# Six query chunks in place of five, a last head set in two halves, and a PSUM bank for P·V taken at its first product, in a fused attention and MLP block

## The chip, the cores and the metric

The kernel runs on one core of one Trainium2 chip. A core has five engines that run side by side, each in the order of its own program: TensorE (PE; its weight loads, PEld, overlap its products), VectorE (DVE), ScalarE (ACT), GpSimd (POOL) and SyncE (SP, which here only issues DMAs). They meet through semaphores. PE writes into PSUM, here eight banks of 128 partitions x 512 fp32; the other data lies in SBUF. The metric is the device time of one execution in microseconds, median of several runs.

## The reference

A transformer block with adaptive layernorm: 2048 tokens, width 640, 32 heads of 20, an MLP of width 1536 with a bilinear gate.

```python
mod = (silu(c) @ w_mod).reshape(c.shape[0], 6, 1, -1)
sa, ca, ga, sb, cb, gb = (mod[:, 0], mod[:, 1], mod[:, 2], mod[:, 3], mod[:, 4], mod[:, 5])
h = layernorm(x) * (1 + ca) + sa
q, k, v = split_heads(h @ wqkv)                 # 32 heads of 20
p = softmax(einsum('bhqd,bhkd->bhqk', q, k) * 20 ** -0.5)
x = x + ga * (merge_heads(einsum('bhqk,bhkd->bhqd', p, v)) @ wo)
h = layernorm(x) * (1 + cb) + sb
x = x + gb * (((h @ w_gate) * (h @ w_up)) @ w_down)
```

## The kernel before

The program is not written out by hand. `build_kernel` makes tasks (engine, estimated duration, dependencies, priority, and at times a gate), and `Sched` plays them through in a list simulation on the host; the order in which it starts them on each engine becomes that engine's instruction stream (`emit_program`), with semaphore waits where a task depends on another engine. So every number of the planner sets an order, and a task that comes late on the chip delays all that stands behind it on its engine.

*Queries* are worked in chunks (`CHUNKS`: 512, 512, 512, 256, 256). Heads go in sets of four, so there are 5 x 8 = 40 items (chunk, head set), in that order. For an item the scores of all 2048 keys are needed. The work is cut into units of 128 keys x 512 queries, or 256 keys x 256 queries (two products side by side, L1480): 64 units for an item of a 512-query chunk and 32 for one of 256. Four heads sit in four 32-row groups of PE's array.

*Exponentials* are made in two ways. Most units go in pairs through ScalarE: one call reads two banks of scores (sets A and B, banks 0 and 1, 3 and 4) and writes bf16 probabilities into a ring `PP` (L1517; `score_q`, one group for each call, NG groups). The others, in quads of four units whose number for each item is in `QUADS` (108 in all), are made by VectorE from the bits of a scaled score: L1541 reads one score bank into `DB`, L1573 and L1581 cut out mantissa and exponent, and L1578 (VectorE) or four pieces of L1593 (GpSimd) multiply; this gives two terms, so P·V runs twice for such a unit. Their scores ride along with a score group (`d_attach`) when their due time (`D_LEAD`, `DL`) has come.

*P·V* (L2038, `pv_issue`) sums over all keys of an item into one PSUM bank, fixed: `BPV` = 7. V carries a column of ones, so the softmax sum comes along. When the last product of an item is done, VectorE transposes the bank into `OT` (L1665, T1), takes reciprocals (L1669), GpSimd normalises (L1671, VectorE for the last item), VectorE transposes back into `OcT` (L1679), and SP copies the heads' rows into `Ocp` (L1692). Only then may the next item's first P·V product start: `st_pv["free"]`.

*After an item row* (all eight sets of a chunk) `suffix` makes the chunk's MLP part: output projection with `wo` (for the last chunk the last head set's part comes straight from `OcT` with `wo7`), residual add into `xck` (L1763), statistics and layernorm (L1777 to L1784; the power -0.5 on GpSimd, L1782), transposes (L1796) with scale and shift into `h2T` (L1801 or L1803), twelve rounds of gate and up with weights that stream through three buffers `stg` (L1836), or that lie ready in `stx` for the last chunk, gate copied to `gsb` and multiplied into `hprod` (L1858 to L1896), and the down products (wd) with a final add (L1919) and the store (L1928). On PE this is all filler ("X" rounds) between score groups: `pick_pe` takes a score group when its banks are free, else P·V candidates, else X rounds by priority, where gates (`GATE_F`) keep a round back until so many exponential groups are out. X rounds and VectorE's score units share the PSUM banks `G` = 5, 6, 2. Dummy products (`do_fill`, L2405; `zero_fill`, L2377) are put in where the recent PE activity falls under `FILL_MIN` or `FILL_Z`. The last chunk's gate and up and down products use the whole array (L935); all others are split in four column groups (L939).

*At the start* x is loaded, normalised, transposed, and projected: K, Q directly or as packed rows that go through DRAM (`kq_round`, `packed_round`; `K_ALL`, `Q_DIRECT`, `LATEQ`), V in two parts of 320 columns (`V_PARTS`, `v_round`, L1288 casts).

`STAGE` overrides planner constants for one item after the other, by item number.

Of the kernel before, what the change touches and what calls it, by code (L numbers as in the profile page):

```python
# [12 lines left out]
SEM = 60.0  # L13
# [21 lines left out]
class Task:  # L35
    __slots__ = ("head", "hval", "hknow", "eng", "dur", "lat", "deps", "emits", "ctr", "prio", "gate", "acq", "on_start", "slots",
                 "start", "done", "needed", "val", "know", "nleft", "ready", "users", "name", "mode", "seq", "rt", "sem",
                 "nbytes", "cond", "alt", "land", "lk")

    def __init__(self, eng, dur, emits, deps=(), ctr=None, prio=0.0, lat=None, gate=0, acq=(), on_start=None,  # L40
# [26 lines left out]
        self.lk = 0  # L67
        if lat is None:
            lat = {"pe": PE_DRAIN, "act": ACT_LAT, "dve": DVE_LAT, "pool": 60.0}.get(eng, 0.0)
        self.lat = lat  # L70

# [49 lines left out]
class Sched:  # L121
# [32 lines left out]
    def locked(self, eng, task):  # L154
# [4 lines left out]
        if task.lk == 2:  # L159
            tt = max(self.t, self.free_at["dve"])  # L160
            for d in sorted(self.readyl["dve"], key=lambda x: (x.prio, x.seq)):
# [89 lines left out]
    def pull(self, eng):  # L251
        p = self.pend[eng]
        while p and p[0][0] <= self.t:
            _, _, task = heapq.heappop(p)
            self.readyl[eng].append(task)

    def step_engine(self, eng):
# [4 lines left out]
        rl.sort(key=lambda x: (x.prio, x.seq))  # L262
        for k, task in enumerate(rl):
            if task.gate > self.progress or (task.cond is not None and not task.cond()):
                continue
# [12 lines left out]
    def steal(self):  # L278
# [4 lines left out]
        for task in self.readyl["dve"]:  # L283
            if task.alt is not None and (best is None or (task.prio, task.seq) < (best.prio, best.seq)):
                best = task
        if best is None or self.free_at["dve"] <= self.t and best is min(self.readyl["dve"], key=lambda x: (x.prio, x.seq)):
# [41 lines left out]
def emit_program(nc, sched, nsem_dma=56):  # L328
# [97 lines left out]
    with nc.Block() as block:  # L426
# [20 lines left out]
        def _(e):  # L447
# [4 lines left out]
CHUNKS = ((0, 512), (512, 512), (1024, 512), (1536, 256), (1792, 256))  # L452
QUADS = ((0, 4, 3, 3, 3, 4, 4, 4),
# [35 lines left out]
K_ALL = (0,)  # L489
# [6 lines left out]
V_PARTS = [[0, 4], [4, 8]]  # L496
# [24 lines left out]
OPFIRST = 0  # L521
# [4 lines left out]
LATEQ = (3,)  # L526
LATEQ_A = 2
LATEQ_F = 0.534
# [4 lines left out]
    0: {"X_LATE": -179.96, "D_RES": 74, "EAGER": 9, "PVMAX": 14, "HOLD": 95, "PVTOL": 249, "D_LATE": 16, "PVMIN": 2, "PVCAP": 12, "FILL_MIN": 4190.746, "TPRIO": 0.75, "XDPRIO": 1.343, "XBACK": 0, "STEAL_GAP": 200, "FILL_Z": 3300.0, "Z_LATE": 0.0},  # L533
    1: {"HOLD": 91, "D_LATE": 10, "PVMAX": 7, "Z_LATE": 89.79, "FILL_MIN": 4705.4},
    2: {"DL": 0.376, "D_LATE": 17, "D_RES": 29, "FILL_Z": 3209.68, "EAGER": 9, "FILL_MIN": 4297.75},
# [1945 lines left out]
```

## Time and profile before

| | us |
|---|---|
| median of 3 runs | 811.79 |
| runs | 810.24 to 813.02 |
| profiled execution: span | 809.0 |
| first exponential (L1517) starts | 16.13 |
| last exponential ends | 770.19 |
| PE busy from 16.1 to 770.2 in dummy products L2405 | 27.5 |
| longest idle of ScalarE before 770 (35.80, after a score) | 1.29 |

The profiled execution is one execution with the profiler on; its span runs from the first to the last instruction. In the stretches shown below each engine's busy time stands with its number of instructions in brackets, then the granted TensorE clock as a share of full speed, the busy share of the DMA engines and GB/s. In a timeline a row has start, duration, engine, line, operation, what it writes and reads, its count, and in square brackets how long the engine had been idle and what ended that. Two successive instructions of one engine overlap, so a mean duration is longer than the step from one to the next.

### The profile page before, as it was taken

The numbers are of one execution on the slowest core, as the hardware profiler recorded it, in microseconds if no ns is written. First come the engines' busy times: TensorE is split into PE (matmuls) and PEld (weight loads), VectorE is DVE, ScalarE is ACT, GpSimd is POOL, SyncE is SP. The second block draws the span as 40 slices with busy tenths as digits, with TensorE's granted clock in tenths as the row PEclk, the third lists the DMA queues.
The fourth block names the chain that finished last, engine by engine and source line by source line (L and its number), as shares of the span: only waits on it lengthen the run. The fifth ranks groups of instructions, "written<-read, shape, count | busy, mean of one in ns | idle before, by whom it ended". The sixth has DMA issues, their size and how long they took to land.

```text
span 809.0 us, 29314 instructions
## 1 busy us (share of the span) xinstructions
PE 792.6 (98%) x12585; PEld 303.1 (37%) x12585; DVE 703.1 (87%) x1273; ACT 763.8 (94%) x853; POOL 321.2 (40%) x330
## 2 busy tenths in 40 slices
PE   9999999999999999999999999999999999999998
PEld 4433333222232333233233232343244433444567
DVE  7979987999999999999998999999699875778973
ACT  7899999999999999999999999999999999999912
POOL 3304244565524442164335334444265340443520
PEclk9999999999999999999999999999999999999999
DMA  9633211113330144100301221001201236005520
GB/s 306 210 87 105 71 46 42 47 36 123 91 67 25 40 112 132 26 9 20 85 25 31 48 57 30 11 22 53 56 6 31 55 78 144 23 30 125 115 70 17
DMA packets 116447, 54.74 MB, mean 68 GB/s; under 512 B 83915, under 2 KB 116319, under 8 KB 116319
## 3 DMA queue, kind: packets, MB, share of 16 engines
q1 hardware_dynamic: 115391, 51.72, 24.3%
q8 instruction: 100, 1.64, 0.8%
q10 hardware_dynamic: 928, 1.15, 0.4%
q14 instruction: 28, 0.23, 0.1%
HBM read 41.85 MB, written 8.41 MB: 62 GB/s over the span
## 4 chain that ended last, share of the span: by engine, by line
PE 52%; ACT 34%; DVE 8%; issue 4%; SPq 1%; DMA 0%; POOL 0%; ACTq 0%; POOLq 0%
ACT PP L1517 34%; PE ps_all L1480 17%; PE ps_all L939 15%; PE ps_all L2038 11%; DVE DB L1541 3%; PE ps_all L935 3%; PE ps_all L1199 3%; PE ps_all L1135 1%; PE ps_all L2403 1%; DVE DSS L1581 1%; DVE DSS L1578 1%; PE ps_all L2405 1%; DVE DSS L1573 1%; PE ps_all L1096 1%; DVE wd L1463 0%
## 5 line engine op out<-in xcount | busy, mean ns | idle before, releaser
L1517 ACT ACTIVATE PP<-ps_all 128x1024 bf16<-128x1024 f32 x808 | 743.9, 1144 | 5.2 <-PE ps_all L1480 4.4
L1593 POOL TENSOR_TENSOR DSS<-DB,DSS 128x512 bf16<-128x512 bf16 x224 | 254.9, 1156 | 324.6 <-DVE DSS L1581 236.0
L1541 DVE TENSOR_SCALAR DB<-ps_all 128x512 int16<-128x512 f32 x432 | 288.5, 684 | 45.0 <-PE ps_all L1480 42.2
L1480 PE MATMUL ps_all<-QT,KT 32*128 32x512 bf16 (+1 forms) x2560 | 315.7, 340 | 8.3 <-ACT PP L1517 5.9
L1480 PEld LDWEIGHTS ps_all<-QT,KT 32*128 32x128 bf16 x2560 | 82.4, 91 | 266.3 <-ACT PP L1517 230.0
L2038 PE MATMUL ps_all<-PP,Vf 128*32 128x512 bf16 (+1 forms) x2032 | 158.8, 343 | 0.3 <-DVE OT L1665 0.3
L939 PE MATMUL ps_all<-h2T,stg 128*32 128x512 bf16 (+1 forms) x1744 | 118.1, 345 | 1.2 <-DVE DB L1541 0.9
L2038 PE MATMUL ps_all<-DSS,Vf 128*32 128x512 bf16 (+2 forms) x1056 | 84.4, 343 | 0.4 <-POOL DSS L1593 0.2
L1573 DVE TENSOR_SCALAR DSS<-DB 128x2048 int16<-128x2048 int16 x108 | 75.5, 699 | 0.5
L1581 DVE TENSOR_SCALAR DSS<-DB 128x2048 int16<-128x2048 int16 x108 | 75.8, 702 | 0.0
L2038 PEld LDWEIGHTS ps_all<-PP,Vf 128*32 128x32 bf16 x2032 | 44.6, 94 | 78.4 <-issue 72.1
L1671 POOL TENSOR_TENSOR OTn<-OT,invT 128x512 bf16<-128x512 f32 (+1 forms) x39 | 37.8, 970 | 89.4 <-DVE invT L1669 89.3
L1578 DVE TENSOR_TENSOR DSS<-DB,DSS 128x2048 bf16<-128x2048 bf16 x52 | 67.1, 1290 | 0.2
L939 PE MATMUL ps_all<-wd,hprod 128*32 128x320 bf16 (+1 forms) x1348 | 60.1, 282 | 0.0
L939 PEld LDWEIGHTS ps_all<-h2T,stg 128*32 128x32 bf16 x1744 | 37.2, 95 | 35.7 <-issue 23.6
L939 PEld LDWEIGHTS ps_all<-wd,hprod 128*32 128x32 bf16 x1348 | 29.7, 96 | 19.7 <-issue 11.3
L2038 PEld LDWEIGHTS ps_all<-DSS,Vf 128*32 128x32 bf16 (+1 forms) x1056 | 26.4, 95 | 19.7 <-issue 8.2
L939 PE MATMUL ps_all<-wV,hT 128*32 128x320 bf16 (+1 forms) x692 | 31.7, 291 | 0.0
L1885 DVE CAST gsb<-ps_all 128x512 bf16<-128x512 f32 x36 | 24.5, 680 | 8.1 <-PE ps_all L939 8.0
L1199 PE MATMUL ps_all<-hT,wq 128*32 128x512 bf16 x375 | 31.5, 382 | 0.0
L1665 DVE STREAM_TRANSPOSE OT<-ps_all 128x512 f32<-128x512 f32 (+1 forms) x40 | 24.1, 603 | 7.3 <-PE ps_all L2038 7.3
L939 PE MATMUL ps_all<-wo,Ocp 128*32 128x320 bf16 (+1 forms) x648 | 29.8, 283 | 0.6 <-DVE DB L1541 0.2
(124 smaller groups left out, 531.6 us busy)
## 6 DMA issues: line engine op xcount, KB each, us to landing
stg<-in_B_w_gate_dram SPq DMA_DIRECT2D x50, 160.0 KB
stg<-in_B_w_up_dram SPq DMA_DIRECT2D x50, 160.0 KB
QT<-q_rows SPq DMA_DIRECT2D x22, 128.0 KB
KT<-k_rows SPq DMA_DIRECT2D x84, 32.0 KB
wm<-in_w_mod_dram SPq DMA_DIRECT2D x3, 800.0 KB
x<-in_A_x_dram SPq DMA_DIRECT2D x7, 320.0 KB
xck<-in_A_x_dram SPq DMA_DIRECT2D x3, 640.0 KB
wd<-in_B_w_down_dram SPq DMA_DIRECT2D x1, 1920.0 KB
```

Of the source, the lines that this page charges most:

```text
L939: return lambda e, b: e.matmul(ps[32 * x:32 * x + 32, b, c0 + o:c0 + o + w], lhs()[:, 32 * x:32 * x + 32], rhs() if w == n else rhs()[:, o ...
L1199: f = [lambda e, b_, k=k, x=x: e.matmul(ps[x:x + min(32, w - x), b_, :], wx[:, k, r0 + x:r0 + min(x + 32, w)], hT[tc][:, k, :], tile_posit ...
L1480: ems.append(lambda e, i=i, kt=kt: e.matmul(dstf()[:, i * u.n:(i + 1) * u.n], KT[32 * u.s:32 * u.s + 32, u.j, kt * 128:(kt + 1) * 128], QT ...
L1517: return e.activation(PPs[g % 2][:, cellp["p"], 0:nu * 512], ps[:, b0:b0 + nu, :].rearrange("p b c -> p (b c)"), AFT.Exp, scale=ESCALE)
L1541: return e.tensor_scalar(DBl[st_["slot"]][:, x * 512:(x + 1) * 512], bank(cell["b"]), EBIAS, 0.0, op0=ALU.add, op1=ALU.max)
L1573: return e.tensor_scalar(DSl[st_["ss"][0]][:, :], DBl[st_["slot"]][:, :], 0x7F, 0x3F00, op0=ALU.bitwise_and, op1=ALU.bitwise_or)
L1578: return e.tensor_tensor(d, DBl[st_["slot"]][:, :].bitcast(BF16), d, ALU.mult)
L1581: return e.tensor_scalar(DSl[st_["ss"][1]][:, :], DBl[st_["slot"]][:, :], 0x7F80, 2, op0=ALU.bitwise_and, op1=ALU.bitwise_or)
L1593: return e.tensor_tensor(d, DBl[st_["slot"]][:, x * w:x * w + w].bitcast(BF16), d, ALU.mult)
L1671: f3 = lambda e: e.tensor_tensor(OTn[:, 0:n].rearrange("p (b c r) -> p b r c", c=32, r=2), OT[:, 0:n].rearrange("p (b r c) -> p b r c", c= ...
L1885: f = lambda e: e.tensor_copy(gsb[:, gs, 0:n], ps[:, r.b["b"], 0:n])
L2038: ems.append(lambda e, i=i, kt=kt, stt=stt, stp=stp: e.matmul(ps[32 * s:32 * s + mc, BPV, 0:u.n], Vf[:, (kt * H + 4 * u.j + s) * VW:(kt * ...
```

## The change

The chunks become 512, 512, 256, 256, 256, 256 with a new `QUADS` (104 quads in all). The last chunk's last head set is made as two items of 128 queries (units of four products of 128 keys x 128 queries), without quads; the output projection, layernorm, transposes, gate/up and down of the last chunk are made for each 128-query tile by itself. The bank for P·V is no longer fixed: bank 7 joins the pool `G`, an item takes a bank when its first P·V product is issued, and the next item may start while the one before is still open (`PV_OPEN`), if `PV_KEEP` banks are free. V is made in four parts of 160 columns. Odd chunks get a second residual buffer `xckb`. The output projection comes earlier in priority (`OPFIRST`), the rows of K for the first 512 tokens are no longer made directly (`K_ALL`), two query blocks come late (`LATEQ`), zero fills are gone, `GATE_F` and `STAGE` are rewritten (the latter from 40 rows of many overrides to some 30 rows of few). The scheduler's own lists are kept sorted, and abandoned alternatives are marked dead; this is host work.

```diff
-CHUNKS = ((0, 512), (512, 512), (1024, 512), (1536, 256), (1792, 256))
-QUADS = ((0, 4, 3, 3, 3, 4, 4, 4),
-         (3, 5, 2, 4, 3, 4, 4, 4),
-         (4, 2, 4, 4, 4, 4, 4, 4),
-         (1, 2, 1, 2, 2, 1, 1, 2),
-         (0, 2, 1, 1, 3, 0, 3, 2))
+CHUNKS = ((0, 512), (512, 512), (1024, 256), (1280, 256), (1536, 256), (1792, 256))
+QUADS = ((0, 4, 3, 3, 3, 4, 4, 4), (3, 5, 2, 4, 3, 4, 4, 4), (2, 1, 2, 1, 2, 1, 2, 1), (2, 1, 2, 1, 2, 1, 2, 1), (2, 2, 1, 2, 2, 2, 1, 2), (2, 1, 2, 2, 2, 1, 2, 0))
+SPLITJ = 1
+QHALF = ((0, 0), (0, 0))
+TB_GATE = 2
+PV_W4 = 430.0
+PV_OPEN = 2
+PV_KEEP = 2
...
-K_ALL = (0,)
+K_ALL = ()
...
-V_PARTS = [[0, 4], [4, 8]]
+V_PARTS = [[0, 2], [2, 4], [4, 6], [6, 8]]
...
-GATE_F = (0.446, 0.693, 0.969, 0.658, 1.0)
+GATE_F = (0.446, 0.6, 0.5, 0.5, 0.5, 1.0)
...
-FILL_Z, Z_LATE = 3300.0, 0.0
...
-OPFIRST = 0
+OPFIRST = 1500
...
-LATEQ = (3,)
-LATEQ_A = 2
-LATEQ_F = 0.534
+LATEQ = (2, 3)
+LATEQ_A = -20
+LATEQ_F = 0.35
...
+    xckb = at("xckb", [128, 4, D], BF16, qt_off)
...
-    G = Slots([5, 6, 2] if HEADG else [5, 6], "G")
+    G = Slots([5, 6, 2, 7], "G")
...
-    BPV = 7
...
+    if SPLITJ:
+        del items[-SPLITJ:], spans[-SPLITJ:], nqs[-SPLITJ:]
+        for hf in range(2):
+            for x in range(SPLITJ):
+                items.append((NC - 1, NSET - SPLITJ + x))
+                spans.append((128 * hf, 128))
+                nqs.append(QHALF[hf][x])
...
+        xfree = outs_r[ci % 2] + v_last
+        if ci % 2 and not alt:
+            xck = xckb
+            xfree = outs_r[1] + sfx_done["qd0"] + x0_done
...
+                gt = gate(KD * 320)
+                if early and SPLITJ:
+                    gt = NG - TB_GATE
...
+            for tl in range(ntl):
+                for f2 in range(0, FT, 2):
+                    mms = []
+                    for w_ in range(2):
+                        for x in range(2):
+                            cell = gu_w[f2 + x][0][w_]
+                            for k in range(KD):
+                                f = full(128, lambda k=k, cell=cell: cell["t"][:, k, :],
+                                         lambda k=k, tl=tl: h2T[:, k, tl * 128:(tl + 1) * 128], k == 0, k == KD - 1,
+                                         256 * w_ + 128 * x)
+                                mms.append((C128, f))
...
     def pv_candidates(t, maxn):
-        it = st_pv["item"]
-        if it >= len(items):
-            return []
-        for d in st_pv["free"]:
-            if d.done is None or d.done + SEM > t:
-                return []
...
+        for it in range(st_pv["item"], min(len(items), st_pv["item"] + PV_OPEN)):
+            info = item_info[it]
+            if info["bank"] is None:
+                ga = G.avail()
+                if ga is None or ga[0] > t or it > st_pv["item"] and len(G.free) < PV_KEEP:
+                    break
...
+            if info["bank"] is None:
+                info["bank"], rel = G.take(G.avail()[1], 1)
+                deps = deps + rel
```

More of the change, by code (lines that the diff above doesn't have):

```diff
@@ L70, in __init__, with KEY @@
         self.lat = lat
+def KEY(x):
+    return (x.prio, x.seq)
 class Slots:
@@ L1933, in suffix @@
         bd["tr"] = tr_l[-1:]
-        bd["out"] = outs
+        if not alt:
+            outs_r[ci % 2] = outs
     t1s = {}
@@ L2031, in pv_emit @@
         ems = []
-        mc = VW if (4 * u.j + s) % 16 == 15 else 32
+        mc = VW if s == 3 and u.j + 1 in [b for _, b in V_PARTS[:-1]] else 32
+        bk = item_info[it]["bank"]
         for i, kt in enumerate(u.kts):
@@ L2103, in pv_issue @@
         sc.free_at["pe"] = sc.pe_end
-        if info["left"] == 0:
-            t1 = t1s[it]
-            t1.deps = [last]
-            sc.left -= 1
-            sc.add(t1)
-            st_pv["free"] = [t1]
+        for it in sorted(last):
+            if item_info[it]["left"] == 0:
+                t1 = t1s[it]
+                t1.deps = [last[it]]
+                sc.left -= 1
+                sc.add(t1)
+        while st_pv["item"] < len(items) and item_info[st_pv["item"]]["left"] == 0:
             st_pv["item"] += 1
```

367 lines of the change are left out of this document (204 added, 163 removed).

## The prediction

> **What bounds the kernel now.** I read the page's head first, then the busy time by stretches (all instructions, then the exponentials of L1517 alone), then ScalarE's and the last 45 us of the whole timeline.
>
> ```profile
> span 809.0 us, 29314 instructions
> PE 792.6 (98%) x12585; PEld 303.1 (37%) x12585; DVE 703.1 (87%) x1273; ACT 763.8 (94%) x853; POOL 321.2 (40%) x330
> L1517 ACT ACTIVATE PP<-ps_all 128x1024 bf16<-128x1024 f32 x808 | 743.9, 1144 | 5.2 <-PE ps_all L1480 4.4
> ```
>
> The exponentials are ScalarE's whole load: 743.9 us for 808, so 0.92 us each (they overlap, hence the longer mean of one). ScalarE idles 5.2 us before them in all.
>
> ```profile
> 630.00:770.20 140.20, 140.10 (x2986) 65.18 (x2986) 107.77 (x201) 139.73 (x151) 52.08 (x54) 1.00 0.35 82
> 770.20:809.00 38.80, 34.89 (x538) 27.69 (x530) 20.34 (x50) 6.24 (x16) 3.21 (x4) 1.00 0.16 43
> 16.10:78.90 62.80, 54.05 (x59) 1.00 0.50 145
> 78.90:560.00 481.10, 480.08 (x524) 1.00 0.20 51
> 630.00:770.20 140.20, 139.73 (x151) 1.00 0.35 82
> ```
>
> The first two lines are all engines (PE, weight load, DVE, ACT, POOL busy; clock; DMA), the last three L1517 alone. Three stages: a start in which 62.8 us hold only 54.05 us of exponentials, 8.75 lost; a body at 481.1/524 = 0.918 us each, rising to 140.2/151 = 0.928 in the 256-query chunks, where PE is busy all the time; and a tail of 38.8 us with none. The granted clock is 1.00 everywhere.
>
> ```profile
> 766.42 3.77 ACT L1517 ACTIVATE PP<-ps_all 128x1024 bf16<-128x1024 f32 x4 [0.41 <-PE ps_all L1480]
> 764.65 0.44 DVE L1665 STREAM_TRANSPOSE OT<-ps_all 128x256 f32<-128x256 f32 x1
> 770.44 3.74 SPq L1692 DMA_DIRECT2D Ocp<-OcT  x5
> 769.57 2.26 PE L939 MATMUL ps_all<-h2Tt,stg 128*32 128x256 bf16 x76
> 775.22 0.44 DVE L1665 STREAM_TRANSPOSE OT<-ps_all 128x256 f32<-128x256 f32 x1
> 775.35 2.08 PE L935 MATMUL ps_all<-wo,Ocp 128*128 128x320 bf16 x14 [0.39 <-DMA Ocp<-OcT]
> 779.07 4.53 PE L939 MATMUL ps_all<-wd,hprodt 128*32 128x320 bf16 x128
> 783.53 0.73 PE L1796 MATMUL ps_all<-ident,xn2c 128*128 128x128 bf16 x10
> 786.34 11.09 PE L935 MATMUL ps_all<-h2Tc,stx 128*128 128x256 bf16 x100
> 799.45 6.71 PE L935 MATMUL ps_all<-wd,hprodc 128*128 128x320 bf16 x60
> 803.43 3.46 SPq L1928 DMA_DIRECT2D out_dram<-xckc  x2
> 9.86 1.28 PE L1096 MATMUL ps_all<-ident,xn 128*128 128x128 bf16 x20
> ```
>
> The last exponential ends at 770.2; call that E. The last head set's sums are read out only at E+5.0 (775.22), because its two quads still go through VectorE. Normalisation and transposes last until E+16.1, gate/up 13.1 us (786.34 to 799.45), down 6.7, and 2.8 pass from PE's last product (806.16) to the end. In the hole before gate/up PE does what the fourth chunk had left: from E some 3 us of its gate/up and 6.8 of its down (200 products in fours at 0.136).
>
> **The change, part by part.**
> *Exponentials.* The quad table falls from 108 to 104 quads. 16 units move from VectorE to ScalarE: 816 calls instead of 808, at the body's 0.918, **+7.3 us**. All lies on ScalarE, which is full. VectorE loses 16 x 0.684 + 4 x 1.40 and pays some 9 for narrower evacuations; it had slack, so 0.
>
> *256-query chunks.* The third chunk's 196 calls become 208 in two halves. At 0.928 they cost 208 x 0.010 = +2.1 more. But that rate is from a stretch where two chunks' MLPs fell together. 560 to 630, with fills (dummy products of L2405 where PE has nothing else), has about 0.909 (77 steps in 70.0), which gives -1.9. Take **+1.0**: work is spread more evenly, but narrow products are back to back. 24 more weight transfers of 160 KB and some 28 more key-row loads of 0.43 us on SP are hidden by SP's gaps and by a DMA share of 0.35; uncovered, PE waits as it did once here (0.5 us).
>
> *Start.* With V in four parts the first head set needs 160 columns of V in place of 320: 16 tiles x 5 steps x (301 - 234 = 67 ns, the means of 320- and 160-wide V products) = 5.4 us of PE leave it, and keys of the first 512 rows pack into 5 rounds in place of 7 (2.2 us). In return 32 more evacuations. The lost time is 8.75 us, of which 3.6 is other ScalarE work (four 0.43 V casts among it). Bounds 0 and -8.75; I take **-3**, half of the V time, since some of the holes wait for layernorm rather than PE.
>
> *PV bank at first product, two sets open.* PE waits 0.3 us in all for a PV bank to be read out (L2038 behind L1665). Gain 0. The price is that two banks may be held, leaving two of four for evacuated rounds where three were free: 0 while the second is held briefly, rival 3 otherwise. The removed zero fill (L2377) issued nothing in this trace: 0. The second residual buffer and the earlier output projection (OPFIRST 1500) only move work: in this trace one half-product of the fourth chunk's came at 691 and the rest at 730, behind the third chunk's down (694 to 726). That let 10 us of MLP slip past E. The third chunk's gate/up and down (24 rounds x 1.08 + 96 x 0.136 = 39 us of PE) went into 617 to 726. The fifth chunk has half of that and 95 us of exponentials (104 calls) to lie beside, so it should be done before E.
>
> *Tail.* The two 128-query halves have no quads; 8 calls each, so the first half's last ends at E-7.4 and the seventh set's at E-14.7. Here the seventh set's Ocp rows landed (775.3) 10.65 us after its read-out (764.65), which came 5.5 after its last exponential. Same lags give E+1.4, without quads and weight issues ahead on SP perhaps E-6; I take E-2. First tile: projection 12 x 0.136 = 1.6, last add 0.5, statistics 0.9, the power 0.55 and scale 0.45 with their hops some 3 altogether, transposes and five short evacuations 1.5, so gate/up starts at about E+4 (E+1 to E+7). It is 120 products; at the 56 ns pace of the 128-wide transposes ((1.28 - 0.22)/19) 6.7 us. Second tile: read-out at E+1, the before's 775.22-to-784.99 chain without its second tile gives ready at about E+9, in time. So E+4 + 6.7 + 1 for the second tile's projection and transposes + 6.7 + 6.7 down + 2.9 to the end = E+28. Bounds: E+25.6 (the second tile's E+9 decides) and E+31. **38.8 to 28.0, -10.8** (-13.2 to -7.8). PE issues in order: where the Ocp rows come later than the schedule has it, the last scores stand behind the waiting projection, and ScalarE behind them; one such wait was 0.39 here.
>
> No row has a 128-wide gate/up product. Bounds are the transpose's 56 ns and, if the weight load decided, the 256-wide 109 ns (then no tail gain in PE time: +12.8). I take 56: a transpose also loads 128x128 weights for each 128 columns. [...]
>
> **Sum**: +7.3 + 1.0 - 3 - 10.8 = -5.5, a span of 803.5. The profiled span of 809.0 is 2.8 below the runs' median, so **806.3 us**.
>
> **The rivals.**
> 1. *PE relief is worth more.* With 10 us less collision and smaller early rounds the start loses 2 in place of 8.75 (-6.8) and 256-query calls go at 0.909 (-1.9 on the new ones, -2.8 on 150 old ones); with the tail 7.3 - 6.8 - 4.7 - 10.8 = -15: 797. For it: the holes of 16 to 61 us all end on PE. Against: 13 of the lost us lie in the well-filled body and need not move. 0.12.
> 2. *The tail keeps its leftovers.* The chunk before last still has 10 us of MLP after E, the hole now holds some 4, and its first gate/up starts at E+7: 31 + 6 = 37. Sum 7.3 + 1 - 3 - 1.8 = +3.5: 815. Against: the balance above. 0.11.
> 3. *Shared banks slow the body: slower than before.* The second open PV set leaves two banks; score pieces for VectorE and projection rounds each hold one for a round and its evacuation, so the in-order PE finds fewer pieces that fit between two scores and the score comes late. The price is the crowded pace on the 600 calls of the quieter body: counted by steps between calls, 140.2/150 = 0.935 for 481.1/523 = 0.920, +9.0. Sum +3.5: 815.3. From 0.009 us a call it eats the gain. For it: in 630 to 770 PE is at 100% and 0.928. Against: VectorE has four quads less. 0.15.
> 4. *Weight loads bound the narrow products.* One load takes 98 ns here and hides behind a 109-ns product in the last gate/up; behind a 56-ns one it may not. If the load sets the pace, 240 x 42 ns = +10.1, 816.4. Against: the transposes. 0.05. [...]
>
> **How the numbers follow.** My case holds 0.55 (own range 801 to 811), 0.02 none of these; the predicted time is its. 0.3% is 2.4 us, about what can be told from no change here. Faster: nearly all of my case (0.49) and rival 1, 0.61. Same: the upper edge of mine and the lower ones of rivals 2 and 4, 0.09. Slower: the rest of rivals 2 to 4 and of mine, 0.30. The range reaches to rival 1 and past rival 3: 797 to 818.
>
> **What would show it.** 816 exponentials, first at about 16, the last ending near 774 to 777; 62.8 us of start holding over 54 us of them. After E no down product of the fifth chunk, gate/up of the first tile 4 us after E in 128-wide products 56 ns apart, a tail of 28. Wrong if the exponentials' pace past 79 us is over 0.927, if the narrow products are 80 ns apart or more, or if the tail exceeds 33.

## The result, and the profile after

The changed kernel takes 822.06 us (median of 4 runs, 821.17 to 825.3) against 811.47 before: 1.0138 times as long, 95% interval 1.0116 to 1.016. Forecast were 806.3 us and "faster". The profiled execution has a span of 819.4 us where before it was 809.0: 10.4 us to account for.

From the head of the page of the changed kernel and its groups (busy time, mean of one, idle time before and what ended most of it):

```profile
span 819.4 us, 34126 instructions
PE 794.0 (97%) x14871; PEld 346.1 (42%) x14871; DVE 686.0 (84%) x1338; ACT 769.2 (94%) x853; POOL 350.1 (43%) x362
L1531 ACT ACTIVATE PP<-ps_all 128x1024 bf16<-128x1024 f32 x816 | 753.1, 1086 | 10.2 <-PE ps_all L1494 9.4
L944 PE MATMUL ps_all<-wo,Ocp 128*32 128x320 bf16 (+1 forms) x692 | 30.5, 278 | 4.1 <-DMA Ocp<-OcT 3.0
```

The exponentials (now L1531) are 816 as planned, and ScalarE's idle time before them has doubled, from 5.2 to 10.2 us. TensorE's output projection (L944) now waits 3.0 us for a transfer.

The stretches that answer to those shown of before; first all engines, then L1531 alone:

```profile
630.00:784.09 154.09, 150.93 (x3606) 78.48 (x3608) 124.44 (x246) 153.48 (x167) 60.46 (x61) 1.00 0.38 84
784.09:819.40 35.31, 32.58 (x611) 27.21 (x610) 18.60 (x52) 4.16 (x11) 1.14 (x2) 0.99 0.10 30
16.10:78.90 62.80, 56.55 (x61) 1.00 0.55 159
78.90:560.00 481.10, 474.70 (x516) 1.00 0.21 55
630.00:784.09 154.09, 153.48 (x167) 1.00 0.38 84
```

The start holds 56.55 us of exponentials where it held 54.05. The body from 78.9 to 560 has lost: 516 calls for 524, and 6.4 us in which ScalarE makes none, against 1.0. The last exponential ends at 784.09, 13.90 later than before, and the tail behind it is 35.3 us against 38.8. So the 10.4 us are 13.9 of exponentials and body, less 3.5 of tail.

Where the body loses is read from the start of the n-th exponential, compared with the same call of before (plus is later). The last two columns belong to the experiments e8 and e12 told below.

| call | changed kernel, us | e8: projection held and residual early | e12: queries first as well |
|---|---|---|---|
| 50 | -2.63 | -3.25 | -3.05 |
| 75 | -0.84 | +0.39 | -2.95 |
| 100 | -0.15 | +1.21 | -2.22 |
| 200 | -0.06 | +1.53 | -0.13 |
| 225 | +0.21 | +1.78 | +0.57 |
| 250 | +4.54 | +1.70 | +0.57 |
| 575 | +5.15 | +1.87 | +1.19 |
| 625 | +7.28 | +1.92 | +1.24 |
| 807 | +6.54 | +0.77 | +1.48 |

The loss comes in steps, not by pace: 4.3 us between calls 225 and 250, 2.1 between 575 and 625; and the lead of the start goes between calls 50 and 100. Between the steps the calls keep the pace of before: from call 250 to 575 they lose 0.6 us, 0.002 us a call. Behind call 807 stand eight calls more, 7.35 us. The first step, in the timeline of the changed kernel (TensorE, ScalarE and SP's queue in order of time):

```profile
235.30 1.26 SPq L1250 DMA_DIRECT2D q_rows<-KPB  x2
236.67 1.76 SPq L1272 DMA_DIRECT2D QT<-q_rows  x4
237.09 0.40 PE L2154 MATMUL ps_all<-PP,Vf 128*32 128x512 bf16 x4
238.47 0.76 SPq L1714 DMA_DIRECT2D Ocp<-OcT  x1
240.47 0.46 PE L944 MATMUL ps_all<-wo,Ocp 128*32 128x320 bf16 x8 [2.98 <-DMA Ocp<-OcT]
240.86 0.39 PE L1494 MATMUL ps_all<-QT,KT 32*128 32x512 bf16 x2
241.29 2.15 ACT L1531 ACTIVATE PP<-ps_all 128x1024 bf16<-128x1024 f32 x2 [2.75 <-PE ps_all L1494]
241.84 0.55 PE L1494 MATMUL ps_all<-QT,KT 32*128 32x512 bf16 x3
```

The last copy of the first chunk's head rows (L1714) is issued at 238.47, behind six query transfers that take SP from 235.30 to 238.43; the rows themselves had been ready since 229.54, the end of VectorE's transpose, and three of the four copies had gone out from 232.55. TensorE has come to the output projection that reads it and waits 2.98 us; the next scores (L1494) stand behind it in the same queue, and ScalarE idles 2.75 us. In the kernel before the same rows were issued and read without a wait, in SP's and TensorE's timeline:

```profile
223.22 1.51 SPq L1692 DMA_DIRECT2D Ocp<-OcT  x2
227.16 0.59 PE L939 MATMUL ps_all<-wo,Ocp 128*32 128x320 bf16 x12
```

There SP had 5 query transfers between 219 and 239 us; in the changed kernel it has 24.

Behind the wait in the changed kernel something follows that the waits don't show: a score product that took 0.39 us takes 0.55. The windows of the changed kernel around that place (PE, weight load, DVE, ACT, POOL busy; granted clock; DMA share; GB/s), cut at the edges of the clock's steps, and the same for the step at 585 us and for a wait at 89 us:

```profile
238.49:241.90 3.41, 1.43 (x29) 0.61 (x29) 0.18 (x2) 0.67 (x2) 1.15 (x1) 1.00 0.37 102
241.90:245.31 3.41, 3.41 (x38) 0.96 (x36) 3.09 (x6) 2.46 (x3) 0.00 (x0) 0.51 0.28 73
245.31:248.73 3.42, 3.42 (x70) 1.40 (x68) 2.83 (x6) 3.12 (x4) 1.18 (x2) 0.99 0.29 81
583.29:586.70 3.41, 2.19 (x54) 1.07 (x50) 2.57 (x7) 2.91 (x5) 1.44 (x2) 1.00 1.14 230
586.70:590.11 3.41, 3.41 (x58) 1.49 (x50) 1.26 (x2) 2.41 (x3) 3.05 (x3) 0.50 0.14 26
88.30:91.71 3.41, 2.47 (x68) 1.41 (x70) 2.22 (x7) 2.11 (x3) 0.00 (x0) 1.00 0.09 26
```

After the wait TensorE gets half its clock for 3.41 us, twice: at 241.95 and at 586.69. ScalarE loses again there: of the 4.3 us of the first step 2.98 are the wait, of the 2.1 of the second 1.22. All the waits of TensorE on transfers behind the start that the view names as such are in this answer of the changed kernel's waits (total, times, longest); the 1.52 us at 89 us stand in it under ScalarE, and that they were for query rows is what e12 below shows:

```profile
PE ps_all L944 <- DMA Ocp<-OcT: 3.0, 1, 3.0
PE ps_all L944 <- DMA stg<-in_B_w_up_dram: 1.2, 1, 1.2
PE ps_all L944 <- DMA xckt<-in_A_x_dram: 1.0, 1, 1.0
```

The second line is the wait at 585, for weights. There the share of the DMA engines was full (1.14, at 230 GB/s, in the window from 583.29), which it was not at 240 (0.37).

And the tail, in TensorE's timeline of the changed kernel, with E = 784.09 for the end of the last exponential:

```profile
789.24 1.18 PE L940 MATMUL ps_all<-h2Tc,stx 128*128 128x128 bf16 x18
790.43 1.41 PE L944 MATMUL ps_all<-wd,hprodt 128*32 128x320 bf16 x36
792.15 5.48 PE L944 MATMUL ps_all<-wd,hprodt 128*32 128x320 bf16 x156
797.57 4.75 PE L940 MATMUL ps_all<-h2Tc,stx 128*128 128x128 bf16 x82
803.27 5.75 PE L940 MATMUL ps_all<-h2Tc,stx 128*128 128x128 bf16 x100
809.97 6.71 PE L940 MATMUL ps_all<-wd,hprodc 128*128 128x320 bf16 x60
```

The first tile's gate/up starts at E+5.2, is broken off after 18 products, and goes on at E+13.5: all 192 down products of the fifth chunk lie between, with 80 of its gate/up ahead of them. The narrow products themselves go at (5.75 - 0.22)/99, about 56 ns (0.22 us is one product from start to end).

### The profile page after: what moved, and what is told of

Same layout as the page of the kernel before. It is cut to its first block, busy times and chain, and to the rows that moved or that the text cites. A ratio compares the mean times of both kernels' runs of the same rounds, so it can differ in the third digit from the quotient of the medians.

```text
span 819.4 us, 34126 instructions
## 1 busy us (share of the span) xinstructions
PE 794.0 (97%) x14871; PEld 346.1 (42%) x14871; DVE 686.0 (84%) x1338; ACT 769.2 (94%) x853; POOL 350.1 (43%) x362
## 4 chain that ended last, share of the span: by engine, by line
PE 55%; ACT 26%; DVE 11%; issue 4%; DMA 3%; SPq 1%; POOL 0%; DVEq 0%; ACTq 0%
ACT PP L1531 26%; PE ps_all L1494 18%; PE ps_all L944 18%; PE ps_all L2154 13%; DVE DB L1555 3%; PE ps_all L940 3%; DMA x<-in_A_x_dram 2%; PE ps_all L1204 2%; DVE DSS L1595 1%; DVE DSS L1587 1%; DVE st L1045 1%; DVE DSS L1592 1%; SPq L1714 1%; DMA stg<-in_B_w_up_dram 0%; DVE hT L1109 0%
## 5 line engine op out<-in xcount | busy, mean ns | idle before, releaser
L1531 ACT ACTIVATE PP<-ps_all 128x1024 bf16<-128x1024 f32 x816 | 753.1, 1086 | 10.2 <-PE ps_all L1494 9.4
L1607 POOL TENSOR_TENSOR DSS<-DB,DSS 128x512 bf16<-128x512 bf16 x248 | 281.9, 1158 | 320.0 <-DVE DSS L1595 259.8
L1494 PE MATMUL ps_all<-QT,KT 32*128 32x256 bf16 (+2 forms) x3136 | 321.6, 308 | 12.4 <-ACT PP L1531 9.0
L1494 PEld LDWEIGHTS ps_all<-QT,KT 32*128 32x128 bf16 x3136 | 89.6, 92 | 239.7 <-ACT PP L1531 183.5
L2154 PE MATMUL ps_all<-PP,Vf 128*32 128x256 bf16 (+2 forms) x2520 | 166.9, 311 | 0.0
L944 PE MATMUL ps_all<-h2T,stg 128*32 128x256 bf16 (+2 forms) x2260 | 124.7, 306 | 1.7 <-DMA stg<-in_B_w_up_dram 1.2
L2154 PE MATMUL ps_all<-DSS,Vf 128*32 128x256 bf16 (+1 forms) x1232 | 85.6, 315 | 0.5 <-DVE DSS L1592 0.3
L2154 PEld LDWEIGHTS ps_all<-PP,Vf 128*32 128x32 bf16 (+1 forms) x2520 | 49.8, 94 | 82.1 <-issue 76.4
L1693 POOL TENSOR_TENSOR OTn<-OT,invT 128x256 bf16<-128x256 f32 (+1 forms) x47 | 39.0, 830 | 66.1 <-DVE invT L1691 65.8
L944 PEld LDWEIGHTS ps_all<-h2T,stg 128*32 128x32 bf16 x2260 | 52.1, 96 | 30.2 <-issue 19.2
L944 PE MATMUL ps_all<-wd,hprod 128*32 128x320 bf16 (+1 forms) x1328 | 61.6, 283 | 0.0
L944 PE MATMUL ps_all<-wV,hT 128*32 128x160 bf16 x1280 | 37.2, 234 | 0.4
L944 PEld LDWEIGHTS ps_all<-wd,hprod 128*32 128x32 bf16 x1328 | 30.0, 96 | 16.0 <-issue 10.4
L944 PE MATMUL ps_all<-wo,Ocp 128*32 128x320 bf16 (+1 forms) x692 | 30.5, 278 | 4.1 <-DMA Ocp<-OcT 3.0
L1686 DVE STREAM_TRANSPOSE OT<-ps_all 128x256 f32<-128x256 f32 (+2 forms) x49 | 25.7, 525 | 10.1 <-PE ps_all L2154 9.9
L1204 PE MATMUL ps_all<-hT,wk 128*32 128x512 bf16 (+1 forms) x360 | 31.8, 382 | 0.2
```

The source lines that it names most:

```text
L944: return lambda e, b: e.matmul(ps[32 * x:32 * x + 32, b, c0 + o:c0 + o + w], lhs()[:, 32 * x:32 * x + 32], rhs() if w == n else rhs()[:, o ...
L1204: f = [lambda e, b_, k=k, x=x: e.matmul(ps[x:x + min(32, w - x), b_, :], wx[:, k, r0 + x:r0 + min(x + 32, w)], hT[tc][:, k, :], tile_posit ...
L1494: ems.append(lambda e, i=i, kt=kt: e.matmul(dstf()[:, i * u.n:(i + 1) * u.n], KT[32 * u.s:32 * u.s + 32, u.j, kt * 128:(kt + 1) * 128], QT ...
L1531: return e.activation(PPs[g % 2][:, cellp["p"], 0:nu * 512], ps[:, b0:b0 + nu, :].rearrange("p b c -> p (b c)"), AFT.Exp, scale=ESCALE)
L1607: return e.tensor_tensor(d, DBl[st_["slot"]][:, x * w:x * w + w].bitcast(BF16), d, ALU.mult)
L1686: t1 = Task("dve", n * 1.1 + 70, lambda e: e.transpose(OT[:, 0:n], ps[:, item_info[it]["bank"], 0:n].rearrange("p (b q r) -> p b r q", q=3 ...
```

## The experiments

Two theories stood against each other. A: the body loses because the new order has TensorE reach work whose transfer is not in yet, and the tail because the fifth chunk's MLP is made late; both are matters of order, so mending the order must bring the time back. B: the changed work itself (more calls, shared banks, narrower chunks, the split) costs what was lost, and a mended order only moves it. Four kernels came first. "Tail" in all that follows is the profiled span less the end of its last exponential.

**e1: the fifth chunk's residual load, layernorm and transposes no longer wait for the fourth chunk's stores.** In the changed kernel the load of `xckt` is issued at 721.71, behind the fourth chunk's last stores at 708.34 and 715.34, and the projection that needs it runs from 725.1, though that chunk's last bank was read out at 699.9.

```diff
+        fq = list(sfx_done["qd1"]) if ci == NC - 2 else first
-                   (first if alt else xfree), prio=15, ...
+                   (fq if alt else xfree), prio=15, ...
```

> The changed kernel, but the residual load, layernorm and transposed activations of the fifth chunk no longer wait for the fourth chunk's stores (only its gate/up products, whose buffer overlaps, still do). Theory A (the tail keeps 9 us of the fifth chunk's MLP because that chunk's residual load waited for the stores; PE had slack, it ran dummy products from 710 to 745): the fifth chunk's projection comes near 711 in place of 727, no product of its down is left after the last exponential, the tail falls from 35.3 to 26 to 28 us, the last exponential stays within 1 us of 784; 812 to 816. Rival B (PE is full before the end, so the leftover only takes score slots): the tail falls but the last exponential comes later by as much, 820 to 823.

820.29 us (817.28 to 822.74), ratio 1.0109 (1.0081 to 1.0137): the size of B. Yet the tail did most of what A said: the load is issued at 668.8, the projection runs from 710.0, 116 down products of the fifth chunk (A had none) and no gate/up are left behind E, and the tail is 30.7 us in place of 35.3 (A: 26 to 28). Of these 4.6 us the body took back 2.7: E came at 786.80. SP's, ScalarE's and TensorE's instructions are in the same order as in the changed kernel up to 668 us, and there this execution lost 4.1 us between calls 50 and 100 where the other lost 2.5, 4.9 for 4.3 between 225 and 250, and nothing at 585, where TensorE's wait for weights was 0.54 us and ScalarE had none. So the places of the waits are the order's, and their size is that execution's. At call 625 the two are level again (6.94 and 7.28 us behind before), so the 2.7 us were lost later: 2.0 of them between calls 752 and 764, in a half-clock stretch that no wait for a transfer precedes. The windows of e1 around it, in the columns of the windows above:

```profile
728.05:731.46 3.41, 2.83 (x47) 1.05 (x40) 3.19 (x8) 3.41 (x5) 1.59 (x2) 1.00 0.38 99
731.46:734.87 3.41, 3.41 (x52) 1.45 (x54) 2.38 (x4) 2.41 (x4) 0.71 (x1) 0.50 0.75 169
```

This run alone doesn't decide between A and B. The pair of e8 and e9 below differs by the same edit, and there E is only 0.3 us later, the tail 5.8 us shorter and the time 5.3 us less, as A has it.

**e2: the planner takes every transfer to land 2 us later.**

```diff
-DMA_LAT = 1700.0
+DMA_LAT = 3700.0
```

> The changed kernel, planned with 2 us more for each DMA's landing (DMA_LAT 3700 in place of 1700). Theory A (the body lost 6.5 us to four places where PE waits for a DMA that lands later than planned, with scores queued behind, two of them followed by a 3.4 us window at half clock): no wait of PE for a DMA over 0.5 us between 80 and 730, no half-clock window, the 807th exponential call starts 4 to 6 us earlier; 815 to 819. Rival B (the crowded PE and the shared banks set the body's pace): the pieces move, the 807th call starts within 1.5 us of now; 820 to 824.

831.73 us (829.95 to 837.57), ratio 1.0242 (1.0225 to 1.0259), beyond both ranges. No wait of TensorE for a transfer over 0.3 us is left between 9 and 800 us, so the edit did its part; but call 807 comes later than in the changed kernel (9.25 us behind before) and not 4 to 6 us earlier, there is a half-clock stretch of 10.24 us from 445.16 although no gap of TensorE in the window before it is over 0.53 us, and the fifth chunk's work was pushed out whole. The profiled execution is the slowest of its runs (837.57). TensorE's timeline of this kernel, E = 786.79:

```profile
795.21 1.69 PE L2487 MATMUL ps_all<-ident 128*32 128x512 bf16 x28
796.73 3.45 PE L944 MATMUL ps_all<-h2Tt,stg 128*32 128x256 bf16 x120
807.23 6.70 PE L944 MATMUL ps_all<-wd,hprodt 128*32 128x320 bf16 x192
```

Behind the last exponential it still makes gate/up of the fifth chunk and dummy products (L2487) beside it, and the tail is 49.0 us. A margin on every transfer is no remedy.

**b104: the kernel before with 104 quads, all four taken from its third chunk.** Nothing else of the change is in it.

```diff
-         (4, 2, 4, 4, 4, 4, 4, 4),
+         (4, 2, 3, 4, 3, 4, 3, 3),
```

> The kernel before with 104 quads in place of 108 (four fewer in the third chunk), so 816 exponential calls. Theory A (every call is on the path): last exponential 7.3 us later, 817 to 820. Rival B (PE limits, and PE has less to do with fewer quads): 811 to 815.

823.76 us (823.75 to 823.9), ratio 1.0154 (1.0138 to 1.0169): 12.1 us on 811.62 beside it, beyond A's range as well as B's. Up to call 807 it keeps step with before within 0.6 us. On the spans (822.0 to 809.0) the eight more calls then take 7.2 us, 3.3 go mostly into one hole, and 2.5 into a longer tail (41.3 to 38.8). ScalarE's timeline of this kernel:

```profile
767.11 6.71 ACT L1517 ACTIVATE PP<-ps_all 128x1024 bf16<-128x1024 f32 x7
776.87 3.77 ACT L1517 ACTIVATE PP<-ps_all 128x1024 bf16<-128x1024 f32 x4 [3.05 <-PE ps_all L2038]
```

The price of the calls is as the sum had it. The hole of 3.05 us ends on TensorE's P·V (L2038) and not on a transfer, so a re-planned end costs something of its own too.

**e5: the last head set whole** (`SPLITJ = 0`).

> The changed kernel with the last head set whole (one item of 256 queries, one MLP of 256 queries as before), all else the same. Theory A (leftover work of the fifth chunk fills the tail, so the split buys almost nothing as it stands): tail 35 to 37, 821 to 824. Rival B (the split already buys most of what it can, about 5 us or more): 827 or more. Rival C (narrow products and two read-outs cost more than they save): under 820.

825.47 us (821.0 to 827.09), ratio 1.0166 (1.0135 to 1.0196). That lies between A's range (821 to 824) and B's (827 or more). Its profiled execution, the shortest of its runs, has E at 782.12 and a tail of 37.1, 1.8 us longer than with the split, as A had it; the medians differ by 3.4 us. The split is worth something, and it is not what made the kernel slow.

None of these four mended the body's first step, so four kernels more went at it.

**e8: e1, with the first chunk's output projection held until 36 exponential groups into the second chunk, in place of 9; e9: the same without e1.**

```diff
-            g = gb + 9 + int((gl - 9) * GATE_F[ci] * rc_[1] / w_tot)
+            g = gb + (9 if ci else 36) + int((gl - (9 if ci else 36)) * GATE_F[ci] * rc_[1] / w_tot)
```

The edit moves the gates of all the rounds of the first chunk's MLP part, those of the projection, which come first, the most.

> The change with the fifth chunk's residual load freed of the fourth chunk's stores (as in the earlier run e1_early_x, 820.29 us), and the first chunk's output projection held back some 12 us, so that its Ocp rows have landed before TensorE reaches it. Theory A: TensorE's in-order queue behind a late transfer is what the body lost, so the 2.4 to 3.0 us wait at 240 us goes, with it the half-clock window behind it, call 250 starts at +1 or less against before instead of +4 to +6, and the time is 815 to 817.5. If the wait at 89 us or at 585 us also opens a half-clock window, about 2 us more each. Rival B: re-planning moves the wait to another transfer (the weights of that chunk's MLP, which now follow the projection more closely): call 250 near 0, but the loss is back by call 350 and the time stays at 819 to 822. Rival C: the loss at 240 is contention of the late query transfers with the scores themselves: call 250 stays at +3 or more.

> The change with only the first chunk's output projection held back some 12 us; the fifth chunk's leftovers stay in the tail. Theory A: 816.5 to 819 us (822.06 less the 4 us of the wait and its half-clock window, with 1 us for what moves), a tail after the last exponential of 34 to 37 us. Rival B (the wait moves): 820 to 823.

e9: 816.62 us (815.46 to 817.72), ratio 1.0064 (1.0039 to 1.009), 5.4 us below the change, E at 778.21, tail 36.8. e8: 811.33 us (809.63 to 815.35, 10 runs), ratio 1.0006 (0.9988 to 1.0024) against 810.93 of before beside it: 10.7 us below the change, better than A's range. SP and TensorE in the timeline of e8:

```profile
240.08 0.77 SPq L1714 DMA_DIRECT2D Ocp<-OcT  x1
251.74 0.65 PE L944 MATMUL ps_all<-wo,Ocp 128*32 128x320 bf16 x16
```

and the window of e8 in which the change had lost:

```profile
237.40:245.00 7.60, 7.27 (x91) 2.00 (x87) 6.57 (x12) 7.60 (x9) 5.29 (x5) 1.00 0.40 108
```

The head rows are no earlier (240.08), but the projection that reads them comes at 251.74, so nobody waits; in that window ScalarE is busy for all 7.60 us (4.22 in the change) at full clock, and TensorE has score work to do instead. Rivals B and C of that expectation fall: the loss did not move, and the late query transfers, which are still there, do not hurt the scores. The wait at 89 us is still there (2.14 us), so call 250 stands at +1.70 and not at A's +1 or less. Both edits together take off more than each alone (1.8 and 5.4): no leftover gate/up, a tail of 31.0, and no step at 240 or 585 us. The step at 585 needs no mending to be smaller: in e1 it was nothing and in e5 0.3 us, with the same order up to there. In e8's tail (E = 778.52) 144 down products of the fifth chunk still go ahead of the first tile, in TensorE's timeline:

```profile
781.39 0.45 PE L1834 MATMUL ps_all<-ident,xn2c 128*128 128x128 bf16 x5
781.77 4.12 PE L944 MATMUL ps_all<-wd,hprodt 128*32 128x320 bf16 x116
786.74 5.76 PE L940 MATMUL ps_all<-h2Tc,stx 128*128 128x128 bf16 x100
793.45 5.75 PE L940 MATMUL ps_all<-h2Tc,stx 128*128 128x128 bf16 x100
800.15 6.71 PE L940 MATMUL ps_all<-wd,hprodc 128*128 128x320 bf16 x60
```

The first tile is transposed by E+3.3, and VectorE has written the last of its activations at E+4.6; its gate/up could follow, but starts at E+8.2.

**e10: e1, with every `Ocp` copy planned 1.3 us later** (`DMA_LAT` plus 1300 where the task's priority is that of `Ocp`).

> As e1_early_x, with every Ocp transfer taken by the planner to land 1.3 us later than it takes it to now, so that all output projections, not the first chunk's alone, stand further behind their rows. Theory A: the projection waits of TensorE are all under 0.3 us, call 250 starts at +1.5 or less, and the time is 815 to 818. Rival B: 820 or more, because the planner's other choices move with it (as the run with 2 us on every transfer, 831.7).

813.92 us (811.0 to 818.99), ratio 1.0036 (1.0013 to 1.0058). Better than A's range, though one projection still waits 0.9 us at 241.9, where A had under 0.3; calls 225 to 250 lose 0.9 us. A margin at the right transfers works where the one on all of them did not.

**e3: the queries of the third 512 tokens back in the first stage** (`LATEQ = (3,)`, `LATEQ_A = 2`, `LATEQ_F = 0.534`, as before the change).

> The change with the query projections of the third 512 tokens back in the first stage, as before it (only the last 512 tokens' are late). Theory A: the SP queue around 225 to 240 us then holds half as many query transfers, the Ocp rows are issued earlier and the wait at 240 us is under 1 us (call 250 within 1.5 us of call 225's lag); the start gives back 2 to 3 us of its gain by call 75: 819 to 821 in all. Rival C (the wait has nothing to do with the late queries): still 2 us or more at the first projection, 823 to 825.

820.06 us (813.57 to 824.29), ratio 1.0101 (1.0046 to 1.0155). A's time, but its reason fell. In the profiled execution, the slowest of the four (824.29), the projection waits 3.41 us at 246.84, because the moved query blocks' transfers now fill the queue at the same hour and the last two groups of head rows are issued at 242.28 and 244.86, again behind loads of queries. As to the late queries this shows nothing either way; in both kernels the last rows stand in SP's queue behind loads of queries.

With e8 equal to before, its own largest remaining loss was the wait at 89 us, where the start's gain goes (calls 50 to 100 in the table). Two kernels went at that wait:

**e11: e8, with the zero rows of the later query scratch written 12 us and more later; e12: that, and the first 512 tokens' query rows ahead of the keys in SP's queue, their projection aimed earlier.**

```diff
-            dur=720.0, gate=WM_GATE + 20 + 12 * tc)]
+            dur=720.0, gate=WM_GATE + 20 + 12 * tc + (40 if tc else 0))]
...
-                [te], prio=1.5, dur=450.0)
+                [te], prio=1.3 if kind == "Q" and tc == 0 else 1.5, dur=450.0)
```

(The first pair is e11's; e12 has 60 for the 40, the second pair, an earlier place for the loads of these rows, `prio` 1.35 for 1.6, and an earlier aim of their projection.)

> As e8_hold, with the writes of zero rows into the query scratch for the later three quarters of the tokens (393 KB each, the first of them issued at 83.7 us, right ahead of the two query loads that the scores wait for at 89 us) moved 12 us and more later; every other instruction keeps its place. Theory A1, the query load is late because it shares the DMA engines with the zeros: the query rows land 1 us or more sooner, TensorE's wait at 89 us is under 1 us, no half-clock window follows, call 100 starts at -1 to 0 against before instead of +1.2, and the time is 807.5 to 809.5. Rival A2, it is late because of its place in the SP queue and of the round trip through memory: the wait stays at 1.5 us or more, 810.5 to 812. A half-clock window behind the wait is worth about 2 us either way.

> As e8_hold, with the zero rows later and the first 512 tokens' query rows written and read back ahead of the key loads in the SP queue, their projection aimed earlier: the two query loads stand 2 us earlier in the schedule. Theory A (both A1 and A2): the wait at 89 us is gone, call 100 starts at -2 to -1 against before, and the time is 806 to 809, below before at 810.9. Rival B: the key loads that now stand behind take the wait over, with a stop of 1 us or more between 90 and 125 us, 810 to 812. Rival C, the start's gain is owed to the same order of the loads: call 50 at -1 or later.

e11: 813.62 us (809.92 to 815.68), ratio 1.0025 (1.0013 to 1.0038). The wait is still 1.73 us (2.14 in e8): A1 falls, the zeros were not the cause. The time is above A2's 810.5 to 812 too. e12: 815.8 us (811.2 to 822.35), ratio 1.0057 (1.0029 to 1.0084). TensorE in e8 at that place, where the profile names no releaser:

```profile
89.23 0.39 PE L1494 MATMUL ps_all<-QT,KT 32*128 32x512 bf16 x3 [2.14 <-issue]
```

and in e12 there and 30 us later:

```profile
87.21 0.39 PE L1494 MATMUL ps_all<-QT,KT 32*128 32x512 bf16 x3
117.69 0.39 PE L1494 MATMUL ps_all<-QT,KT 32*128 32x512 bf16 x3 [1.32 <-DMA KT<-k_rows]
```

The wait at 89 is gone, so it was for the queries, and the scores now wait for keys at 117.7 instead: rival B, though the time is above its 810 to 812. Even so the lead over before is lost. Of the 2.95 us at call 75, 0.13 are left at call 200, with no half-clock stretch in that execution ahead of its end: 0.7 go by call 100, 1.4 at the wait for the keys, 0.5 at 176 us, behind two waits of TensorE for VectorE (0.37 and 0.20 us), and 0.2 after that.

**e13 and e14: e8 with 107 and with 108 quads,** that is 810 and 808 calls.

```diff
-(3, 5, 2, 4, 3, 4, 4, 4), ... (2, 2, 1, 2, 2, 2, 1, 2), (2, 1, 2, 2, 2, 1, 2, 0))
+(3, 5, 2, 4, 4, 4, 4, 4), ... (2, 2, 1, 2, 2, 2, 2, 2), (2, 2, 2, 2, 2, 2, 2, 0))
```

(e13 leaves the fifth row as it is.)

> As e8_hold (811.33 us, 816 exponential calls) with three more quads, one each in the fifth set of the second chunk and in the second and sixth sets of the last chunk: 810 calls. Theory A, a call costs its 0.906 us on the path wherever it stands, as the sum had it: six calls are 5.4 us, 806 to 808, faster than before at 811. Rival B, TensorE and VectorE have no room for the extra quads, so that the calls come further apart: the last exponential ends less than 3 us earlier and the time is 809 to 812. A half-clock window that comes or goes is worth about 1.6 us in one execution and is not counted for either.

> As e13_q107 with a fourth quad, in the seventh set of the fifth chunk: 808 calls, as many as before the change. Theory A: 804.5 to 807, and the gap to before is then the shorter tail and what is left of the start's gain. Rival B: no faster than e13_q107, 808 to 812, since the fifth chunk's MLP is pushed towards the last exponential and the tail takes back what the body gives.

e13: 811.47 us (808.54 to 817.35), ratio 1.0008 (0.9989 to 1.0027). The last exponential ends 4.5 us earlier than in e8 (774.03), so in E the calls are worth nearly their 5.4; the tail is 33.5, 2.5 longer, with 164 down products left, and a wait at 344 us is followed by a half-clock stretch (granted clock 0.50 from 344.49 to 347.90). e14: 815.37 us (810.92 to 820.93), ratio 1.0051 (1.003 to 1.0072), E at 772.88 and a tail of 36.2, with all 192 down products and 44 of gate/up behind E. The time of e13 is rival B's, though not by B's reason: A was right as far as the last exponential, and the tail took it back. e14 is above rival B's 808 to 812, and the tail is why, as B had it. The extra quads bring P·V products to TensorE (two for each unit); that these push out the fifth chunk's MLP fits the products left behind E and was not shown apart. No version beat before.

One reading goes across these runs. Each result lists the mean granted clock of each run, and the times follow it:

| mean clock of the run | e8, us (runs) | e12, us (runs) |
|---|---|---|
| 1.000 | 810.4 (4) | 811.6 (3) |
| 0.998 | 811.7 (4) | 812.8 (2) |
| 0.996 | | 815.8 (2) |
| 0.992 to 0.994 | 815.1 (2) | 818.4 (2) |
| 0.985 to 0.990 | | 821.2 (3) |

One half-clock stretch of 3.41 us lowers the mean over 810 us by 3.41 x 0.5 / 810 = 0.0021, about the step between these rows. A fitted line over e8's ten runs gives 0.73 us for each 0.001, so about 1.5 us for a stretch. That is an estimate of what goes with a stretch, the short supply of work ahead of it included; the loss beyond the wait itself was 1.35 us at 240 (4.33 less 2.98) and 0.9 at 585 (2.13 less 1.22). The changed kernel's runs stand at 0.994 and 0.995, two and a half stretches; before stands at 1.000 in nearly all.

## Why the prediction was wrong, point by point

The terms of the sum, against the changed kernel and against e8, in which the order is mended at two places:

| term | forecast, us | changed kernel | e8 |
|---|---|---|---|
| eight more calls | +7.3 | +7.4 | +7.6 |
| body up to the start of call 807 (chunks +1.0, start -3) | -2.0 | +6.5 | +0.8 |
| tail | -10.8 | -3.5 | -7.8 |
| sum on the span | -5.5 | +10.4 | +0.6 |

Two of the three signs that the prediction gave for being wrong came: past 79 us the exponentials go at 0.934 us each (over 0.927), and the tail exceeds 33. The third, narrow products 80 ns apart, did not.

*The exponentials* were right: 7.4 us, and 7.2 in b104, where nothing else of the change is in.

*The transfers are the step that failed.* The prediction let the added transfers be hidden "by SP's gaps and by a DMA share of 0.35; uncovered, PE waits as it did once here (0.5 us)", and named the late `Ocp` rows with the 0.39 us seen before. Uncovered, TensorE waited 1.5 us at 89, 2.98 at 240 and 1.2 at 585, and the last two were followed by a half-clock stretch, for which the sum had no term: 4.3 and 2.1 us in all. At 240 the share of busy DMA engines was the wrong gauge (0.37 in that window); what decided was the place of one transfer in SP's queue against one instruction in TensorE's. At 585 the engines were full, and whether place or supply made that wait was not tried. The prediction's sentence of what stands behind a waiting projection (the last scores, then ScalarE) was the right mechanism, but it was written for the tail, with a price nearly eight times too small, and the sum had nothing for it in the body. The transfers ahead of the rows there are of the query blocks that the change makes late (`LATEQ`), which the sum doesn't mention; e3 puts one of the two blocks back and the wait stays, so their lateness alone is not shown to be the cause. Holding that projection back, with the MLP rounds behind it, took 5.4 us off (e9), and 9.0 off e1 (e8).

*The start* was right in size where it was looked for (2.6 us at call 50) and wrong as a term of the sum, since the lead didn't last. In the changed kernel 1.6 us of it go at the 89-us wait and 0.7 in the calls from there to 100; what takes these 0.7, which e12 loses too, stays open. The V products that left the start are not the reason as far as the record shows: in the changed kernel 560 of 160 columns stand between 125 and 232 us (164 of 320 before), and from call 100 to 200 it keeps step with before, 0.15 and 0.06 us ahead. TensorE had room for them: the dummy products between 79 and 232 us fell from 56 to 4.

*The tail's pace* was right: 120 products of 128 columns in about 6.7 us a tile, 56 ns each. The forecast had that pace from 20 transposes; it held over 100 products, which took 5.75 us with a load of 128x128 weights for each (200 loads for the 200 products on `stx`, 98 ns a load).

*The tail's content* failed at "so it should be done before E". That counted the fifth chunk's work against the exponentials beside it and not against when it may begin: its residual load stood behind the fourth chunk's stores, and its projection came at 725 with 59 us left. TensorE was meanwhile making dummy products (64 from 715 to 745), so the room was there and was not used. Freed of that, the tail is 30.7 to 31.0 us (e1, e8). The 3 us to the forecast 28 are the fifth chunk's down products that are left: in e8 the first tile's activations are ready at E+4.6, near the forecast E+4, and its gate/up starts 3.6 us later. (The lower bound E+25.6 comes to E+25.3 by its own terms, 9 + 6.7 + 6.7 + 2.9; the forecast does not rest on it.)

*The P·V banks* were rightly costed at nothing: no wait of P·V for a bank is among TensorE's waits. Rival 3, the body slowed by shared banks, priced 0.015 us a call on the quieter body; between the steps the calls lose 0.002 to 0.003 (100 to 225, 250 to 575), and past 630 they go at 154.09/167 = 0.923 against 0.928 before. So it falls, and so does rival 4 (56 ns). Rival 1 falls too: the start still loses 6.25 us (62.8 less 56.55) where it had 2. Rival 2 named the tail as it came out (37 forecast, 35.3 measured, with 80 products of the fifth chunk's gate/up and all its down behind E), and its 815 missed the body.

*The range* left out a body that loses by steps. The profile of before could not show such a loss: behind its start TensorE waited for transfers twice, 0.52 and 0.39 us, both in the tail.

## What to carry to other kernels

In a program whose order is fixed beforehand, ask of each changed order which instruction reads a transfer soon after its issue, what stands behind it on its engine (here scores, behind a wait of 2.98 us), and where that transfer stands in its queue; here a DMA engine share of 0.2 to 0.4 told nothing of that. A lead won in one stage is kept only if the next transfer that a later stage reads moves forward with it; here the start's 2.6 us ran into the wait for the query rows. And a chunk's "time beside it" begins when its inputs may be loaded, so follow the stores and buffers that hold the first load before counting its work as hidden.

## What the runs showed that was not expected

Two of TensorE's waits in the changed kernel had a second price (1.35 and 0.9 us beyond the wait itself). Half-clock stretches begin there at 241.95 and 586.69 us, 344.74 apart. The trace has each of them as 3.413 us long, and 344.74 is 101 times that; in e1 three begin at 89.76, 239.94 and 731.46, apart by 44 and 144 times 3.413. So in both runs the starts stand a whole number of stretch lengths apart, and in the changed kernel not at a fixed distance from the wait (1.48 us behind the end of the one at 240, 1.70 behind that at 585); and the same place in the order may or may not be followed by one: at 89 us waits of 1.70 (e1) and 2.14 us (e8, granted clock 0.51 from 90.60 to 94.02) were, and waits of 1.52 (the changed kernel) and 1.98 (e13) were not. Stretches of two and three times the length occur too (6.83 us in e1 and e3, 10.24 in e2). Whether idle time brings a stretch on, and how much of it, is not settled. Windows of 3.41 us with 1.43 and 2.19 us busy were followed by half clock, one with 2.47 was not, and in e1 (shown above) one with 2.83 and in e11 one with 2.73 were:

```profile
187.10:190.52 3.42, 2.73 (x27) 0.93 (x31) 3.41 (x7) 3.42 (x5) 1.27 (x2) 1.00 0.01 2
190.52:193.93 3.41, 3.41 (x57) 1.51 (x55) 2.75 (x6) 2.85 (x4) 1.90 (x2) 0.50 0.09 23
```

The four windows above that were followed by half clock were not idle but short of work: TensorE was busy for 1.43 to 2.83 of their 3.41 us.
